# Transposing the second chunk's rows on TensorE between projection groups instead of by DMA

## The chip, the cores and the metric

The kernel runs on one core of a Trainium2 chip. The metric is the device time of one execution in microseconds (us). A profile also gives the span from the first to the last instruction; in these runs the time is about 1.8 us above the span (810.66 against 808.9 for the profiled execution of before). The record marks an execution as slow when it is over 1.5% above the fastest of the same kernel.

## The reference, cut to what matters

A block of a transformer: `h = x + attention(layernorm(x)) @ wo`, then `h + down(gate(layernorm(h)) * up(layernorm(h)))`, on 2048 rows of 1024 elements in bf16. Only its start matters:

```python
m = jnp.mean(x, axis=-1); v = jnp.var(x, axis=-1)
xn = (x - m) / jnp.sqrt(v + 1e-5)
qkv = xn @ wqkv                      # [2048,1024] @ [1024,3072]
# sliding, dilated attention over 8 positions follows, then wo, then the feed-forward part
```

## The kernel before

The 2048 rows are handled in four chunks of 512, each of four row tiles of 128. The projection needs the normalized rows transposed, with the feature on the partitions (`lnT`). Chunk 0, at the very start, transposes on TensorE. Chunks 1 to 3 use DMA transposes from the issue queue of SyncE (SP):

```python
class Norm1:
    def stat(self, t):       # VectorE bn_stats; ScalarE log and exp give 1/sqrt(v + eps)
        stats(xtiles[self.c][t], self.mv4, t)
        rstd_of(self.mv4, self.rs4, t, t + 1)
    def norm(self, t):       # VectorE: one tensor_scalar, bf16 row tile
        self.lns[t] = normalize(xtiles[self.c][t], self.mv4, self.rs4, t)
    def transpose(self, t):  # SP: DMA transpose, 128x1024
        ...                  # c = self.c; allocates lnTs[c] at the first row
        nc.sync.dma_start_transpose(lnTs[c][:, :, bass.ts(t, 128)], self.lns[t][:])
```

Side work like this, and attention, is put into generators. After each projection group (8 matmuls, 1.73 us) a small scheduler adds 1.73 us of credit, at most 4 in all, and runs side work until the credit is spent. That fixes the program order on every engine.

```python
def qkv(c, blocks, last=False):
    for b in blocks:
        for j in range(4):
            ps = psum.tile([128, TC], F32, tag="mm", ...)     # 8 banks, handed out in turn
            mm_group(ps, wts["qkv", b], j, lnTs[c])
            evac_qkv(c, b * 4 + j, ps)                        # ScalarE copies, SP stores q, k, v
            bg.step(GROUP_US)
...
bg.add(rows_gen(norm1[1], True))     # chunk 1: statistics, normalization, DMA transposes
rows2 = rows_gen(norm1[2], False)    # chunk 2: its DMA transposes come below
bg.add(rows2)
...
qkv(0, range(1, 4))                  # 12 groups of chunk 0
load_qk(0)
bg.finish(rows2)
for t in range(4):
    norm1[2].transpose(t)
xtiles[3] = load_x(3, "x", nc.sync)
pump(6)                              # weights of blocks 4 and 5
bg.add(stats_gen(norm1[3]), bg.now + 6.0)
start_attention(0)
qkv(1, range(4))                     # needs all of chunk 1's lnT
qkv(0, range(4, 6))
...
```

## Time and profile before

| what | value |
|---|---|
| time, median of the first 3 runs | 808.54 us (808.07 to 808.65) |
| span and mean granted clock of the profiled execution (its time: 810.66) | 808.9 us, 0.996 |
| idle time of TensorE ahead of chunk 1's first group | 4.26 us |
| granted clock from 42 to 50 us | 0.60 |

"Busy" counts an engine's instructions and not its waits; "PE" is TensorE, "PEld" its weight load, "DVE" VectorE, "ACT" ScalarE, "POOL" GpSimd, and "SPq" the issue of DMAs on SyncE. `L379` is line 379 of the kernel. In a group's row the idle time before it stands after the second bar, with what ended it. The lines themselves are in the prediction.

### The profile page before, as it was taken

The page shows a single profiled execution, that of the slowest core. Times are in us where ns is not written, and L with a number is a line of the kernel's source. Part 1 is how long each engine was busy: PE and PEld are TensorE (multiplying, and loading weights), DVE is VectorE, ACT ScalarE, POOL GpSimd, SP SyncE. Part 2 cuts the span into 40 slices and gives each one's busy share as a digit, 9 for nine tenths or more (in the row PEclk, how much of TensorE's full clock was granted, in tenths as well). Part 3 has the DMA queues.
Part 4 walks back from the last instruction along what each step waited for, and adds up shares of the span by engine and source line. Part 5 has one row for each costly group of instructions (what it writes and reads, how often), then busy time and mean ns, then how long its engine had stood idle before and what let it go on. Part 6 is the DMA issues. An engine that isn't in the chain of part 4 may idle for free.

```text
span 808.9 us, 9878 instructions
## 1 busy us (share of the span) xinstructions
PE 794.0 (98%) x3700; PEld 410.3 (51%) x3769; DVE 552.1 (68%) x580; ACT 254.3 (31%) x562; POOL 165.3 (20%) x160
## 2 busy tenths in 40 slices
PE   8889999999999999999999999999999999999998
PEld 5334444444444444444444444466666666644445
DVE  6519999999899998998989926645646556311111
ACT  4516445323333321013333100244555555400000
POOL 0000000200002000010000010597867778000000
PEclk9989999999999999999999999999999999999999
DMA  7998693897956869667637596542313233466500
GB/s 261 249 268 201 167 269 88 265 288 197 330 172 214 286 243 213 213 216 239 202 105 237 172 245 178 130 121 62 104 53 105 68 90 98 158 208 191 179 27 27
DMA packets 195200, 144.32 MB, mean 178 GB/s; under 512 B 83408, under 2 KB 187984, under 8 KB 193104
## 3 DMA queue, kind: packets, MB, share of 16 engines
q1 hardware_dynamic: 191568, 121.66, 53.7%
q0 software_dynamic: 3584, 22.02, 8.3%
q8 instruction: 30, 0.49, 0.3%
q14 instruction: 18, 0.15, 0.1%
HBM read 114.29 MB, written 22.02 MB: 169 GB/s over the span
## 4 chain that ended last, share of the span: by engine, by line
PE 89%; DVE 7%; DMA 2%; issue 1%; ACT 0%; SPq 0%; DVEq 0%
PE ps L379 18%; PE acc L558 15%; PE pg L379 12%; PE pu L379 12%; PE wo L500 7%; PE pz L609 6%; PE py L609 6%; PE px L609 6%; PE pv L609 3%; PE accl L548 3%; DVE pv L462 2%; DMA lnT<-ln 1%; DVE pv L470 1%; PE ps L341 1%; DVE oD L472 1%
## 5 line engine op out<-in xcount | busy, mean ns | idle before, releaser
L379 PE MATMUL ps<-lnT,w_qkv 128*128 128x512 bf16 x721 | 161.3, 383 | 5.2 <-DMA lnT<-ln 4.3
L379 PEld LDWEIGHTS <-w_qkv 128*128 128x128 bf16 x736 | 72.6, 99 | 93.3 <-issue 8.6
L379 PE MATMUL pg<-lnT,w_wg 128*128 128x512 bf16 x439 | 105.0, 379 | 0.5
L379 PE MATMUL pu<-lnT,w_wu 128*128 128x512 bf16 x439 | 104.9, 379 | 0.4
L558 PE MATMUL acc<-w_wd,gs 128*128 128x512 bf16 x439 | 96.7, 379 | 0.5
L540 DVE TENSOR_TENSOR h<-acc,h 128x512 bf16<-128x512 f32 x28 | 17.4, 682 | 91.1 <-PE acc L558 91.1
L290 ACT CAST sg<-ps 128x512 bf16<-128x512 f32 x96 | 55.0, 587 | 68.9 <-PE ps L379 65.4
L462 DVE TENSOR_TENSOR pv<-vD,at 128x4096 bf16<-128x4096 bf16 x32 | 72.5, 2286 | 0.3
L419 DVE TENSOR_TENSOR prod<-qD,kD 128x4096 bf16<-128x4096 bf16 x32 | 72.3, 2283 | 0.1
L379 PEld LDWEIGHTS <-w_wu 128*128 128x128 bf16 x448 | 43.8, 98 | 52.9
L558 PEld LDWEIGHTS <-gs 128*128 128x128 bf16 x448 | 43.8, 98 | 52.9
L379 PEld LDWEIGHTS <-w_wg 128*128 128x128 bf16 x448 | 43.8, 98 | 52.9
L525 ACT CAST gs<-pg 128x512 bf16<-128x512 f32 x56 | 32.9, 588 | 100.0 <-PE pg L379 96.6
L500 PE MATMUL wo<-w_wo,oT 128*128 128x512 bf16 x251 | 55.6, 379 | 0.3
L474 POOL DMA_DIRECT2D od<-oD x4 | 2.2, 542 | 253.1 <-DVE oD L472 253.1
L609 PE MATMUL px<-lnT,w_pair 128*128 128x512 bf16 x210 | 52.5, 380 | 1.0
L585 POOL TENSOR_TENSOR sw<-w_pair 128x512 fp32r<-128x512 bf16 x28 | 36.5, 1304 | 75.6 <-DMA w_pair<-in_B_w_gate_dram 43.3
L530 ACT CAST us<-pu 128x512 bf16<-128x512 f32 x56 | 32.8, 587 | 57.5 <-PE pu L379 54.1
L500 PEld LDWEIGHTS <-oT 128*128 128x128 bf16 x256 | 25.1, 98 | 30.2
L181 ACT ACTIVATE rs<-mv,eps 128x1 f32<-128x1 f32 x32 | 9.5, 296 | 95.5 <-DVE mv L178 91.9
L587 POOL TENSOR_TENSOR sw<-w_pair 128x512 fp32r<-128x512 bf16 x28 | 36.9, 1319 | 0.0
L421 DVE TENSOR_TENSOR prod<-prod 128x4096 bf16<-128x4096 bf16 x16 | 36.6, 2288 | 0.3
(127 smaller groups left out, 1057.9 us busy)
## 6 DMA issues: line engine op xcount, KB each, us to landing
w_wd<-in_B_w_down_dram SPq DMA_DIRECT2D x32, 896.0 KB, 6.3
w_wg<-in_B_w_gate_dram SPq DMA_DIRECT2D x14, 1024.0 KB, 7.1
w_wu<-in_B_w_up_dram SPq DMA_DIRECT2D x14, 1024.0 KB, 5.5
w_wo<-in_A_wo_dram SPq DMA_DIRECT2D x8, 1024.0 KB, 8.0
w_pair<-in_B_w_gate_dram SPq DMA_DIRECT2D x14, 512.0 KB, 4.0
w_pair<-in_B_w_up_dram SPq DMA_DIRECT2D x14, 512.0 KB, 5.3
w_qkv<-in_A_wqkv_dram SPq DMA_DIRECT2D x5, 1024.0 KB, 10.9
kd<-sg SPq DMA_DIRECT2D x32, 144.0 KB, 3.1
```

Source lines behind the costliest of these rows:

```text
L290: nc.scalar.copy(sg[:, HB:HB + TC], ps[:])
L379: nc.tensor.matmul(ps[:], lhsT=wt[:, ko, bass.ts(j, 128)], rhs=rhs[:, ko, :], start=(ko == 0), stop=(ko == KO - 1))
L419: nc.vector.tensor_tensor(prod[:, j], qD[:], kD[:, :, o:o + SUB], ALU.mult)
L421: nc.vector.tensor_tensor(prod[:, :, 0:16], prod[:, :, 0:16], prod[:, :, 16:32], ALU.add)
L462: nc.vector.tensor_tensor(pv[:, j], vD[:, :, o:o + SUB], at[:, w, None, :].to_broadcast((128, DH, SUB)), ALU.mult)
L500: nc.tensor.matmul(ps[:], lhsT=oTs[c][:, kk, t, :], rhs=wts["wo", c, hf][:, kk, :], start=(kk == 0), stop=(kk == KO - 1))
L525: nc.scalar.copy(gs[:], pg[:])
L530: nc.scalar.copy(us[:], pu[:])
L558: nc.tensor.matmul(acc[t][:], lhsT=hT[f][:, bass.ts(t, 128)], rhs=wts["wd", c, hf, b][:, j, :], start=(f == 0), stop=(f == NF - 1))
L585: nc.gpsimd.tensor_tensor(sw[:, 0], a21, a22, ALU.add)
L587: nc.gpsimd.tensor_tensor(sw[:, 2], a11, a21, ALU.subtract)
L609: nc.tensor.matmul(ps[:], lhsT=lhs[:, ko, :], rhs=rhs[:, ko, :], start=(fresh and ko == 0), stop=(ko == 3), skip_group_check=not fresh)
```

## The change

The intent is to take the second chunk's input off the DMA queues, which are busy with stores and loads at that time, and to put it on TensorE, which runs in program order and whose transposes can't be held up by a queue. Each row tile becomes 8 transposes of 128x128 into two banks, one copied out by ScalarE and one by VectorE, one scheduler step after the row's normalization or later.

```diff
+        def transpose_on_array(self, t):
+            ...
+            for hf in range(2):
+                pt = psum.tile([128, KO // 2, 128], BF, tag="mm", name=f"ptb{c}_{t}_{hf}")
+                for kk in range(KO // 2):
+                    nc.tensor.transpose(pt[:, kk, :], self.lns[t][:, bass.ts(4 * hf + kk, 128)], ident[:])
+                copy = nc.vector.tensor_copy if hf else nc.scalar.copy
+                copy(lnTs[c][:, bass.ts(hf, 4), bass.ts(t, 128)], pt[:])
-    def rows_gen(n, transposed):
-        for t in range(5):
+    def rows_gen(n, on_array):
+        for t in range(6):
             if t < 4:
                 n.stat(t)
                 yield 1.5
-            if t > 0:
+            if 0 < t < 5:
                 n.norm(t - 1)
-                if transposed:
-                    n.transpose(t - 1)
                 yield 0.55
+            if t > 1 and on_array:
+                n.transpose_on_array(t - 2)
+                yield 0.45
```

## The prediction

> **What bounds the kernel now.** The page says where to look: TensorE is busy almost everywhere.
>
> ```profile
> PE 794.0 (98%) x3700; PEld 410.3 (51%) x3769; DVE 552.1 (68%) x580; ACT 254.3 (31%) x562; POOL 165.3 (20%) x160
> ```
>
> So only TensorE's own work or its idle time can move the end. Next I read the groups of instructions, for the idle time ahead of TensorE and who ended it. The last columns are busy us, mean ns of one, then idle us and releasers.
>
> ```profile
> L379 PE MATMUL ps<-lnT,w_qkv 128*128 128x512 bf16 x721 | 161.3, 383 | 5.2 <-DMA lnT<-ln 4.3
> ```
>
> That is the only sizeable idle time on TensorE after the start: 4.3 us, once, ended by a DMA transpose into the normalized input. No other TensorE row has more than 1.5 us. Then the stretches around it (busy us of each engine, granted clock, DMA share, GB/s):
>
> ```profile
> 36.00:42.00 6.00, 2.22 (x11) 0.78 (x8) 0.55 (x1) 3.07 (x13) 0.00 (x0) 0.96 1.03 221
> 42.00:50.00 8.00, 7.30 (x21) 2.83 (x23) 0.55 (x1) 1.17 (x2) 0.54 (x1) 0.60 1.29 211
> 50.00:60.00 10.00, 9.95 (x47) 4.51 (x46) 2.75 (x6) 1.67 (x4) 0.00 (x0) 1.00 1.02 301
> ```
>
> TensorE is idle for four of the six microseconds up to 42, and the eight after them run at a mean clock of 0.60. So the wait costs twice: the idle time, and a slow restart. The chain that ended last, in order of time (start, us, what), has the same place:
>
> ```profile
> 34.18 8.05 DMA lnT<-ln
> 42.48 2.29 PE ps L379 x5
> 44.99 12.39 PE ps L379 x49
> 57.44 10.74 PE ps L379 x49
> ```
>
> Five matmuls take 2.29 us there. In full stride a piece of 50 (one record missing) advances 10.79 us, which is 0.2158 us each. The fourth transpose of the second chunk was issued at 34.2 and took 8.1 us to land (the first three took 3.1 to 3.6), since it shares busy queues with the stores of q and k. The second chunk's first projection group waits for it.
>
> **The size of the hole.** The last group of chunk 0's first three blocks ends at 38.22 (the timeline's piece starts at 17.34 and lasts 20.88). The first output-projection matmul starts at 169.67. Between them the program has 24 groups of chunk 1, 8 of chunk 0, 24 of chunk 2 and 16 of chunk 3, which is 72 groups of 8, or 576 matmuls; 576 x 0.2158 = 124.3 us. The stretch lasts 131.45 us. The excess is 7.15 us: 4.26 idle and 2.9 of slow clock. This is all there is to win.
>
> **What the Trainium skill says.** "TensorE: Matmul & The Clock Gate", section "What's actually happening", says that TensorE falls to half clock after an idle window of about 3.4 us, and needs about as long of sustained work to return. The trace agrees: idle for 4.26 us, then matmuls 0.43 us apart until about 48.4. The same page, "Part 4: PE-mode transpose", says that transposes don't count as busy for this gate. The prologue of this kernel speaks for harmlessness here: it puts bursts of eight transposes between matmuls, and from 10 to 18 us the granted clock is 1.00. "VectorE: DVE Perf Modes", section "The three transpose paths", gives 390 ns for a 128x128 transpose on TensorE and 1309 by DMA. In a pipelined burst this trace shows far less on TensorE, and that is the duration I use. "PSUM — Partial Sum Buffer", "Specifications (TRN2)", counts 8 banks; this kernel's pool has 8 and hands them out in turn, which matters below.
>
> **The change part by part.** Removed: four DMA transposes between 28.2 and 42.2, and with them the wait, the slow clock, and the hold of their row buffers (VectorE lost 9.0 us in three waits for those). Gain on the path: 7.15 us.
>
> Added: 4 x 8 transposes on TensorE, all in line with matmuls, so all on the path. The prologue does the very same:
>
> ```profile
> 14.49 0.61 PE L331 MATMUL pt<-ident,ln 128*128 128x128 bf16 x8
> 14.92 0.59 ACT L333 COPY lnT<-pt 128x512 bf16<-128x512 bf16 x1 [1.07 <-PE pt L331]
> 14.94 2.56 PE L341 MATMUL ps<-lnT,w_qkv 128*128 128x128 bf16 x40
> 15.14 0.42 DVE L336 COPY lnT<-pt 128x512 bf16<-128x512 bf16 x1 [0.71 <-PE pt L331]
> ```
>
> From 14.49 to the next matmul at 14.94 is 0.45 us for eight, so 4 x 0.45 = 1.8 us more TensorE work. The copies, 4 x 0.59 on ScalarE and 4 x 0.42 on VectorE, lie beside the matmuls: ScalarE has about 0.6 to 1.0 us of work per 1.73 us group. They do delay what stands behind them.
>
> Where do they land? I played the scheduler that mixes side work between groups by hand (1.73 of credit gained per group; 1.5 spent per row's statistics, 0.55 per normalization, 0.45 per transposed row). Row 0 is transposed after group 4, row 1 after group 5, rows 2 and 3 after group 6. In VectorE's program order the statistics of row 3 now stand behind the copy of row 0, which waits for TensorE, and the normalizations of rows 2 and 3 behind those. In the kernel before, VectorE ran them ahead of TensorE:
>
> ```profile
> 22.68 1.28 DVE L177 BATCH_NORM_STATS2 st<-x 128x6 f32<-128x512 bf16 x2
> 23.99 0.21 DVE L178 BATCH_NORM_AGGREGATE mv<-st 128x2 f32<-128x12 f32 x1
> 24.11 0.49 DVE L186 TENSOR_SCALAR ln<-x,mv,rs 128x1024 bf16<-128x1024 bf16 x1
> ```
>
> From these statistics to the end of that normalization is 24.11 + 0.49 - 22.68 = 1.92 us. In the changed kernel (an estimate from these rows) group 4 ends at 24.24, 0.2 before its eviction at 24.44 in the timeline. Row 0's transposes start there; VectorE's copy starts 0.65 later, as in the prologue (14.49 to 15.14), at 24.9; the statistics of row 3 at about 25.25, row 2 is normalized by 27.2, and row 3, after the copy of row 1 and its own ScalarE step, by about 28.1. TensorE reaches row 2 at 24.24 + 2 x (0.45 + 1.73) = 28.6. So TensorE doesn't wait, by about half a microsecond. The banks don't hold it either: a transposed row takes 2 of 8, and the allocation eight back is always an eviction at least two groups old. The second chunk is complete at about 31; its first group starts at 38.22 + 1.8 = 40.0.
>
> Sum: -7.15 + 1.8 = -5.35, from 808.54 to 803.2.
>
> **The rivals.** (1) VectorE takes over as the bound. It is busy almost without a break from 57.2, when the fourth chunk's rows land, to 190, so only an earlier start moves it. Those rows are loaded behind the stores of k and chunk 2's transposes on the same issue queue (issue from 50.2, landing 7.0 us later). In the changed kernel the last k store can't be issued before its group has ended, near 40.0, and been copied, 41.0, which puts the rows' issue near 48 instead of 50.2. So VectorE moves up by only some 2.3 us, TensorE by 5.35. What TensorE needs of it next: the attention output of chunk 0 (last piece issued at 156.7, 6.8 to landing, so 163.5; used at 169.67; slack 6.2) and the second normalization of chunk 0 (last transpose issued at 189.8, 3.2 to landing, so 193.0; first used at 197.3; slack 4.3). The last becomes 4.3 - 5.35 + 2.3 = 1.25. If VectorE didn't move at all, TensorE would wait 1.05 there: 804.3. Later VectorE is ahead again (in the feed-forward part it waits 17 times, 11.2 us in all, for ScalarE's copies of TensorE's results), so the lag isn't carried on. (2) The row normalizations come late and TensorE waits for them in order, after group 6. With half a microsecond of margin, a stall of 1 us is well possible: 804.2. (3) The slow clock comes anyway, because the transposes count as idle: 2.9 us kept, 806.1. The longest stretch is 0.9 us (rows 2 and 3), against 0.45 in the prologue; unlikely. (4) The wait for the transpose is replaced by a wait for weights: blocks 4 and 5 of the projection are issued at 52.9 and land 10.9 and 12.9 us later, at 63.8 to 66.6. Before, the first is used at 42.48 + 2.9 + 128 x 0.2158 = 73.0, now at 67.6, and its issue moves up as well. No stall. (5) The transpose's wait is hidden anyway: no, it is in the chain and the idle time is TensorE's.
>
> **The range and the chances.** The middle is 803.3, a tenth over the sum for rivals 1 and 2. Below, hardly more than the whole 7.15 less 1.8 is to be had, and repeats of the kernel before spread 0.6 us: 802.2. Above, rivals 1 and 2 together give about 805.3, so 805.6 leaves them in. Two per cent is 16 us, more than twice the hole, so faster by that much is practically excluded; slower would need a new wait of over 21 us, which nothing here suggests.
>
> **What would show it.** Right: no idle time on TensorE ahead of the second chunk's first group, clock 1.00 from 36 to 50, 32 more small matmuls of 0.056 us apart near 24 to 30, chunk 1 starting near 40.0, the first output-projection matmul near 164.3 and the rest shifted as a block. Wrong: idle time before the transposes ended by a normalization, before the first gate matmul (near 192) ended by a transpose, or before the output projection; or a clock under 1.00 after the transposes. If that first gate matmul comes 5.35 earlier but the end doesn't, a later wait that no row shows today has taken the gain.

## The result, and the profile after

The changed kernel takes 804.84 us (median of 4, 804.5 to 806.28) against 808.6 of before (median of 4, 808.07 to 810.99). Ratios here and below are taken over the fast runs of the same rounds, so not quite the ratio of the medians. This one is 0.9956, with a 95% interval of 0.9936 to 0.9975: 3.8 us faster by the medians. The number lies inside the predicted range (802.2 to 805.6); the middle, 803.3, was 1.5 too low.

The page of the changed kernel, and its row of projection matmuls:

```profile
PE 797.9 (99%) x3801; PEld 411.8 (51%) x3801; DVE 553.0 (69%) x584; ACT 255.4 (32%) x566; POOL 165.3 (21%) x160
L391 PE MATMUL ps<-lnT,w_qkv 128*128 128x512 bf16 x736 | 159.7, 379 | 0.0
```

The idle time behind the second bar, 5.2 us before, is 0.0. The stretches of the changed kernel (busy us of PE, PEld, DVE, ACT and POOL, then the granted clock, DMA share and GB/s):

```profile
36.00:42.00 6.00, 6.00 (x29) 2.74 (x28) 1.22 (x4) 3.55 (x12) 0.00 (x0) 1.00 0.76 163
42.00:50.00 8.00, 8.00 (x39) 3.63 (x37) 0.00 (x0) 1.77 (x4) 0.54 (x1) 1.00 1.12 230
50.00:60.00 10.00, 10.00 (x48) 4.49 (x46) 5.59 (x13) 1.97 (x7) 0.00 (x0) 1.00 0.93 265
```

TensorE is busy throughout, at a clock of 1.00. Hole and slow restart are gone together. The chain of the changed kernel through the same place (start, us, what):

```profile
17.16 6.91 PE ps L391 x32
24.06 0.45 PE ptb L234 x8
24.51 1.73 PE ps L391 x8
26.24 0.45 PE ptb L234 x8
26.68 1.73 PE ps L391 x8
28.41 0.89 PE ptb L234 x16
29.30 30.86 PE ps L391 x143
```

Transposes stand where the hand-played scheduler put them, after groups 4, 5 and 6. Eight take 0.45 us, and nothing but TensorE is on the chain. The timeline of the changed kernel (start, us, engine, line, operation) shows the step that was tightest:

```profile
24.55 0.42 DVE L236 COPY lnT<-ptb 128x512 bf16<-128x512 bf16 x1 [2.13 <-PE ptb L234]
24.89 1.27 DVE L177 BATCH_NORM_STATS2 st<-x 128x6 f32<-128x512 bf16 x2
27.07 0.54 DVE L186 TENSOR_SCALAR ln<-x,mv,rs 128x1024 bf16<-128x1024 bf16 x1
28.25 1.06 PE L234 MATMUL ptb<-ident,ln 128*128 128x128 bf16 x16
```

VectorE does wait for TensorE in its copy, as predicted, and the last row is normalized at 27.61, 0.64 us before TensorE reaches rows 2 and 3 at 28.25. So TensorE doesn't wait.

To see where the time went I split each profiled span into three parts: the start of the first full projection matmul; the stretch from there to the first output-projection matmul, less its 672 matmuls of 0.2158 us (145.02 us), which I call the loss; and the rest.

| profiled execution | start | loss | rest | span |
|---|---|---|---|---|
| before | 17.34 | 7.32 | 639.22 | 808.9 |
| changed | 16.99 | 1.81 | 639.07 | 802.9 |

The loss goes from 7.32 to 1.81, a gain of 5.51. (The prediction's 7.15 counts from the modelled end of a matmul instead of a start, hence 0.17 less.) The other 0.5 us between the two spans is chance at the start and in the rest. So the two profiles differ by about the predicted 5.35, while the two sets of timed runs differ by 3.8. That gap is what the experiments were for.

### The profile page after: what moved, and what is told of

It is laid out like the page before. It is cut to its first block, busy times and chain, and to the rows that moved or that the text cites. A ratio compares the mean times of both kernels' runs of the same rounds, so it can differ in the third digit from the quotient of the medians.

```text
span 802.9 us, 10008 instructions
## 1 busy us (share of the span) xinstructions
PE 797.9 (99%) x3801; PEld 411.8 (51%) x3801; DVE 553.0 (69%) x584; ACT 255.4 (32%) x566; POOL 165.3 (21%) x160
## 4 chain that ended last, share of the span: by engine, by line
PE 98%; DMA 1%; SPq 0%; DVE 0%; issue 0%
PE acc L570 21%; PE ps L391 20%; PE pu L391 12%; PE pg L391 12%; PE wo L512 7%; PE pz L621 7%; PE py L621 7%; PE px L621 6%; PE pv L621 3%; PE accl L560 3%; PE ps L353 1%; DMA w_qkv<-in_A_wqkv_dram 1%; PE ptb L234 0%; PE pt L343 0%; SPq L269 0%; SPq L272 0%
## 5 line engine op out<-in xcount | busy, mean ns | idle before, releaser
L621 PE MATMUL px<-lnT,w_pair 128*128 128x512 bf16 x224 | 55.6, 381 | 0.0
```

Of the source, the lines that this page charges most:

```text
L621: nc.tensor.matmul(ps[:], lhsT=lhs[:, ko, :], rhs=rhs[:, ko, :], start=(fresh and ko == 0), stop=(ko == 3), skip_group_check=not fresh)
```

## The experiments

The first set of four ran on one chip, the second and third on two others. Each has its own 11 timed executions of before beside it. Their medians were 808.45, 809.68 and 810.95. Theory A says that the profiled execution of before was one of its slower ones; theory B says that the change costs more than its 1.8 us of transposes.

### same: the kernel before against itself

No edit.

> The kernel before, unchanged, against itself, to see how its own time varies. The predicted gain was 5.35 us, the timed one 3.76. Theory A: the profiled execution of before (span 808.9, clock 0.996, time 810.66) was one of its slower ones. The wait of about 4.3 us comes every time, but the slow clock after it (2.9 us) only in some executions[...]. Then the spans of this run's executions fall into two groups, near 806.5 (clock 0.998 or more) and near 809 (clock near 0.996), and their mean is near the timed 808.6 less 1.8. Theory B: the wait and the slow clock come every time and the changed kernel costs more than 1.8 us: then all spans are 808.5 to 809.3 with clock 0.996.

Measured: 809.91 us median (808.18 to 811.52, 6 runs), ratio 1.0009 (0.9981 to 1.0037). The times of its six executions and of the 11 of before beside it, with the mean granted clock:

```
same:   808.18 (0.998) 808.36 (1.000) 808.55 (1.000) 811.27 (0.997) 811.52 (0.996) 811.52 (0.996)
before: 806.17 (1.000) 807.20 (0.998) 807.67 (0.997) 807.75 (0.997) 808.35 (1.000) 808.45 (0.998)
        810.43 (0.998) 810.98 (0.996) 811.49 (0.996) 811.72 (0.996) 811.97 (0.996)
```

Here they fall into two groups with nothing between 808.6 and 810.4, and the upper one mostly has the lower clock. (The two groups are no law: beside the second set four of the 11 executions of before lie between 809.3 and 809.9.) What holds is that before's time spreads over 5.8 us by itself (806.17 to 811.97), and the time of the first profile, 810.66, is in the upper part. That is theory A. The profile of this kernel shows a wait that is not the same as in the first profile (first line, who waited for what: us in total, times, longest; second line, the stretch from 42 to 50 as above):

```profile
PE ps L379 <- DMA kd<-sg: 5.4, 1, 5.4
42.00:50.00 8.00, 5.74 (x20) 2.26 (x21) 0.55 (x1) 1.06 (x2) 0.00 (x0) 0.79 1.24 234
```

The wait is 5.4 us here, and the loss is 7.19 (7.02 counted as the prediction counts), so 1.6 us of slow clock. (The releaser named is the transfer that came last by the records; it is a store of k. The fourth transpose was issued just ahead of it and took 9.1 us to land.) The size of the hole is thus no constant: it depends on when one transfer lands in busy queues, and on how long the slow clock lasts after the wait. By the mean clock from 42 to 50 us, 0.79 here and 0.60 in the first profile, that is about 3.4 us and 6.4 us at half clock, where matmuls come 0.43 us apart instead of 0.2158 (an estimate: 8 x 0.21 / 0.5 and 8 x 0.40 / 0.5), though the wait is the longer one here.

### keep_warm: idle matmuls inside the wait

```diff
     start_attention(0)
+    fill = psum.tile([128, 512], F32, tag="mm", name="fill_ps")
+    for i in range(16):
+        nc.tensor.matmul(fill[:], lhsT=warm[:, 0:128], rhs=warm[:], start=True, stop=True)
     qkv(1, range(4))
```

> Before, with 16 idle matmuls (16 x 0.2158 = 3.45 us) put on TensorE between the last group of chunk 0 and the first of chunk 1, inside the wait of 4.26 us. The DMA transposes stay. Theory A (the slow clock is a result of the idle time, on top of it): idle time falls below 1 us, the clock stays at 1.00 from 42 to 50, and every execution is as fast as before's fastest: spans 805.7 to 806.5, 0.5 to 2 us below before's mean and with less spread. Rival (the clock is low for another reason, or its slowness is absorbed): spans as before, 806.5 to 809. If the idle time, and not the clock, were all that the change wins, this kernel would show no gain at all.

Measured: 809.63 us median (808.46 to 810.4), ratio 1.0003 (0.9976 to 1.0031), the clock 0.999 or 1.000 in all six. The granted clock from 42 to 50 is 1.00 in this kernel's profile; that stretch, and the waits of TensorE:

```profile
42.00:50.00 8.00, 7.44 (x35) 3.45 (x36) 0.55 (x1) 2.10 (x4) 0.54 (x1) 1.00 1.27 212
PE ps L379 <- ACT sg L290: 1.6, 1, 1.6
PE ps L379 <- DMA lnT<-ln: 1.3, 1, 1.3
```

The slow clock is indeed a result of the idle time: filling the wait removes it. But the time did not fall: the spans are 806.6 to 808.5, so my expectation of 805.7 to 806.5 failed and the rival's 806.5 to 809 came. TensorE now came sooner to a second wait that was not in the profile of before: for ScalarE's eviction of a bank, at 65.0 us.

### doubled: each transpose made twice

```diff
-                for kk in range(KO // 2):
+                for kk in [*range(KO // 2)] * 2:
                     nc.tensor.transpose(pt[:, kk, :], ...)
```

> The changed kernel with each of its 32 transposes on TensorE made twice into the same place. If their cost is wholly on the path, as predicted (0.45 us per 8), the time is 1.8 us above the changed kernel's 804.84: 806.6, ratio to before about 0.998. If they cost less (hidden in idle time), it is 804.8 to 805.5; if theory B holds and a row on TensorE costs twice what I took, 808 or more.

Measured: 806.54 us median (806.41 to 807.07), ratio 0.9969 (0.9945 to 0.9993). That is 1.70 us above the changed kernel's 804.84 (a different set of runs) and in its profile the loss is 3.60 against 1.81. The chain shows rows 2 and 3:

```profile
29.31 1.79 PE ptb L234 x32
```

So a transpose costs 0.056 us on the path, wholly and no more, and theory B is out. The clock stayed at 1.00 even through rows 2 and 3, which are now 1.8 us of transposes without a matmul between.

### last_row: only row 3 on TensorE

```diff
                 n.norm(t - 1)
+                if on_array and t < 4:
+                    n.transpose(t - 1)
                 yield 0.55
-            if t > 1 and on_array:
-                n.transpose_on_array(t - 2)
+            if t == 5 and on_array:
+                yield "later", 3.0
+                n.transpose_on_array(3)
                 yield 0.45
```

> Rows 0 to 2 of the second chunk by DMA as before (they landed at 31.4, 33.4 and 36.4, ahead of the need at 38.2), only row 3, the one that the wait was for, on TensorE. If the wait is the fourth transfer's alone, the whole gain stays at a quarter of the cost: 3 x 0.45 = 1.35 us below the changed kernel, so about 803.5, no idle time before the second chunk. Rival: one of the first three transfers, still queued among the stores, becomes the last to land and the wait comes back at 1 to 4 us: 805 to 808.

Measured: 808.78 us median (805.67 to 809.36), ratio 0.9986 (0.9959 to 1.0013): the expected 803.5 failed, though the wait for the transposes is gone. The timeline of this kernel shows the second wait in full:

```profile
45.78 0.59 ACT L305 CAST sg<-ps 128x512 bf16<-128x512 f32 x1 [1.14 <-PE ps L394]
57.59 1.28 DVE L177 BATCH_NORM_STATS2 st<-x 128x6 f32<-128x512 bf16 x2 [20.45 <-DMA x<-in_A_x_dram]
59.16 0.29 ACT L181 ACTIVATE rs<-mv,eps 128x1 f32<-128x1 f32 x1 [12.79 <-DVE mv L178]
62.38 0.57 ACT L305 CAST sg<-ps 128x512 bf16<-128x512 f32 x1
63.00 3.22 PE L394 MATMUL ps<-lnT,w_qkv 128*128 128x512 bf16 x8 [3.44 <-ACT sg L305]
```

Read it from the top. The first line is the last eviction before the stop. The fourth chunk's rows land at 57.6; VectorE had waited 20 us for them. ScalarE's small instruction on their variance stands in program order ahead of the next evictions, and waits 12.8 us for VectorE. Meanwhile no bank is emptied. Eight banks hold 8 x 1.73 = 13.8 us of TensorE's work, and that is used up: TensorE waits 3.4 us. A DMA load thus stops TensorE by way of two engines. In the changed kernel's timeline the same chain is there, and it just holds:

```profile
46.61 0.59 ACT L302 CAST sg<-ps 128x512 bf16<-128x512 f32 x1 [1.14 <-PE ps L391]
54.27 1.28 DVE L177 BATCH_NORM_STATS2 st<-x 128x6 f32<-128x512 bf16 x2 [16.12 <-DMA x<-in_A_x_dram]
59.05 0.57 ACT L302 CAST sg<-ps 128x512 bf16<-128x512 f32 x1
```

From one eviction to the next are 12.4 us, against 13.8 of banks. The margin is less than the difference: an eviction starts some 0.2 us after its group ends and takes 0.57 us before the bank is free, so about 0.6 us is left (an estimate). The same count for last_row, from the eviction at 45.78 to the one at 62.38, gives a wait of 16.6 + 0.8 - 13.8 = 3.6 us, where the profile has 3.44.

### again: the changed kernel once more

No edit.

> The changed kernel again, on one chip with the next three, for its spread. The 17 executions of before beside the first four experiments ran from 806.17 to 811.97 (mean 809.5), so the 3.76 first measured rests on a lucky handful of before. Theory A: changed near 804.7, most executions within 0.5 us of it, 4 to 5 us below the mean of before on the same chip (ratio 0.994 to 0.996), with single executions 1 to 2 us up, where a second wait shows: the fourth chunk's rows land late, VectorE's statistics wait for them, ScalarE waits in order for these, its evictions stop and TensorE runs out of banks. Theory B (the gain is 3.8 and the rest was never there): ratio 0.9956 or above.

Measured: 805.09 us median (804.91 to 805.33, 5 runs), ratio 0.9941 (0.9927 to 0.9954), so 4.6 us by the medians. The loss in its profile is again 1.81. There was no outlier this time.

### after_later: the fourth chunk's statistics five groups later

```diff
-    bg.add(stats_gen(norm1[3]), bg.now + 6.0)
+    bg.add(stats_gen(norm1[3]), bg.now + 15.0)
```

> The changed kernel with the fourth chunk's statistics put five groups later in program order (ready 15 us instead of 6 us after the first 12 groups), so that ScalarE has evicted more groups before it comes to wait for them. Theory A: no execution is slowed by banks; same fast level (804.5 to 804.9), no outlier over 805.3. Rival (the outlier near 806.3 has another source, say the clock at the start): the outliers stay.

Measured: 807.18 us median (806.17 to 809.08), ratio 0.9968 (0.9953 to 0.9983): 2.1 us slower than the changed kernel beside it. The expectation failed. The loss in the profile is 1.81, so the front is untouched; the rest is 1.1 us longer. TensorE waits 0.9 us at 486 us, for the attention output of the last chunk. The store of that output (engine, operation, out<-in) is issued in this kernel at

```profile
469.54 0.56 POOL L486 DMA_DIRECT2D od<-oD  x1 [102.69 <-DVE oD L484]
```

and in the changed kernel at

```profile
450.74 0.56 POOL L486 DMA_DIRECT2D od<-oD  x1 [87.57 <-DVE oD L484]
```

My edit made the scheduler lose credit (it keeps no more than 4 us while nothing is ready), so attention fell behind in program order until the end, by 19 us at the last chunk. The profiled execution was the fastest of six; that the slower ones have more of the same is likely and not shown.

### last_row_later: only row 3 on TensorE, later statistics

The edits of last_row and after_later together.

> Only row 3 on TensorE, as in the run before of that idea, and the fourth chunk's statistics five groups later. That run had no wait for a transpose, but a wait of 3.4 us for ScalarE's eviction, near 60 us. If this second wait was all that hid the gain, it is gone: 803.3 (the changed kernel's 804.7 less 3 x 0.45), 1.3 to 1.4 us below the changed kernel, ratio to it 0.998. If instead DMA traffic with three transposes left keeps the rows of the fourth chunk so late that another wait appears: 804.5 or more.

Measured: 804.77 us median (804.32 to 805.89), ratio 0.9939 (0.9924 to 0.9953), level with the changed kernel beside it (805.09). The wait for ScalarE is gone and the loss is 0.47, a quarter of 1.81 as it should be. But the edit has after_later's drawback: 1.2 us of wait at 485 us for the last chunk's attention output.

### keep_warm_later: idle matmuls and later statistics

The edits of keep_warm and after_later together.

> Before with the 16 idle matmuls in the wait, and the later statistics. The last such run had no slow clock, but lost 1.6 us to the eviction wait. With that gone, what is left is the wait itself (4.3 to 5.4 us) without the slow clock: 801.1 (the changed kernel less its 1.8 us of transposes, an estimate of the time with neither) plus 4.3 to 5.4, so 805.4 to 806.5 and little spread, some 3 us below before's mean. If it stays at 808.5 or more, the slow clock wasn't a cost of its own.

Measured: 809.69 us median (807.84 to 811.04), ratio 0.9995 (0.9978 to 1.0012), clock 1.000 in all six. The profiled execution is the fastest of the six (span 806.0, the others 806.5 to 809.3). In it the transposes had landed before the idle matmuls ended, so the loss is just the 3.48 of these, and a wait of 0.9 us stands at 488 us, once more from the later statistics. Expected 805.4 to 806.5, so missed, and by the test in the text above (808.5 or more) it counts against a cost of the slow clock. I don't take it as settled, since the edit's own cost is in it (after_later: 2.1 us by the medians); but what made five of the six executions slower than the profiled one was not traced.

### last_row_x3: only row 3 on TensorE, an earlier load

```diff
+    xtiles[3] = load_x(3, "x", nc.sync)
     for t in range(4):
         norm1[2].transpose(t)
-    xtiles[3] = load_x(3, "x", nc.sync)
```

(on top of last_row). The text below takes the late attention output for that of chunk 0; the trace, read again, shows it at 485 us, which is chunk 3, as told above. I had misread it.

> Only row 3 on TensorE, and the fourth chunk's rows loaded ahead of the third chunk's four DMA transposes on the issue queue instead of behind them. The later statistics had only moved the trouble: VectorE starts attention when these rows have landed (57.0 in that run), and the attention output then reached TensorE 1.2 us late. If this chain (rows landed, 92 us of VectorE work, output stored and loaded again) is what limits once TensorE is faster, loading the rows earlier starts VectorE near 50, both waits go, and the time is 803.3 to 803.5, 1.4 below the changed kernel's 804.7 to 805.1, ratio to before 0.9925. Rival: the early load lands in the same busy queues and delays the first chunk's q and k or a row's transpose instead; then 804.5 or more.

Measured: 803.63 us median, ratio 0.9939 (0.9903 to 0.9974), but four executions at 802.48, 803.41, 803.51 and 803.74, and two at 808.77 and 811.9. The profile fell on the slowest, and shows why that one is slow:

```profile
PE ps L394 <- DMA w_qkv<-in_A_wqkv_dram: 5.5, 1, 5.5
```

The rows now land at 47.0 and the wait for ScalarE is gone, but the weights of block 4 stand behind rows and transposes on the issue queue. The four issues of the transposes took 20.5 us (45.15 to 65.63), so the weights were issued at 65.7, landed at 71.8 and came 5.5 us late, and the slow clock comes with that wait: the loss is 8.98.

### keep_warm_x3: idle matmuls, an earlier load

The edits of keep_warm and last_row_x3's load on before.

> Before with the 16 idle matmuls in the wait, and the early load of the fourth chunk's rows. The two runs with idle matmuls kept the clock at 1.00 but lost what that gave to later waits (an eviction, the attention output). If those waits come from the late rows, they are gone here and what remains is the wait for the transposes: 801.1 plus 4.3 to 5.4, so 805.4 to 806.5, 3 to 4 us below before, with little spread. If it is 808.5 or more again, the late rows weren't the reason, or the slow clock is no cost of its own.

Measured: 808.06 us median, ratio 0.9983 (0.9956 to 1.001): three executions at 806.64, 806.79 and 807.09, all with clock 1.000, three at 809.03, 811.07 and 812.27. The profile is of the fast kind: no wait at all, loss 3.48, which is the 16 idle matmuls. The slow kind was not traced; late weights as in last_row_x3 would fit. The expected 805.4 to 806.5 was missed, by the fast kind too, if only by 0.1 to 0.6 us. Its control, before_x3, has the slow clock in its profile and is no slower (mean 808.1 against 808.8).

### before_x3: the earlier load alone

The load of last_row_x3 on before.

> Before with the early load alone, as the control of the two above. In before the profile shows no wait on TensorE behind the late rows, so theory A expects no change but chance: ratio 0.998 to 1.002, with the slow clock (0.996) still there in part of the executions. Rival: part of before's own spread (806 to 812) is the late rows too; then it is 1 to 3 us faster and evener.

Measured: 807.89 us median (806.63 to 810.25), ratio 0.9969 (0.9949 to 0.9989). Faster than I expected, by 2.5 us in the mean. Its profile has a wait of 2.8 us and a loss of 4.65, because the fourth transpose landed 6.4 us after its issue, not 8.1 or 9.1. Yet the early load is issued at 44.4, after that transpose had landed, so I can't see how it could have helped it. Whether this is chance or an effect stays open.

### reorder_x3: no transpose on TensorE, another order

```diff
-    pump(4)
+    pump(5)
     xtiles[2] = load_x(2, "x", nc.sync)
+    pump(6)
...
     load_qk(0)
+    xtiles[3] = load_x(3, "x", nc.sync)
+    qkv(0, range(4, 6))
+    load_v(0)
     bg.finish(rows2)
     for t in range(4):
         norm1[2].transpose(t)
-    xtiles[3] = load_x(3, "x", nc.sync)
-    pump(6)
...
     qkv(1, range(4))
-    qkv(0, range(4, 6))
-    load_v(0)
```

> No transpose on TensorE at all: before with chunk 0's last two projection blocks moved ahead of chunk 1's (their weights loaded ahead of the third chunk's rows, which aren't needed soon), and the early load of the fourth chunk's rows. The second chunk's DMA transposes then have 13.8 us more before they are needed. If the wait is a matter of order alone, it is gone at no cost on TensorE: 801.1 plus at most 0.5, 3 to 4 us below the changed kernel, ratio to before 0.990. Rival: the moved weights come too late (wanted at 38.2 instead of 73) or push the third chunk's rows or the stores back, and a wait of 2 to 5 us appears in another place: 804 to 807.

Measured: 811.73 us median (810.09 to 813.05), ratio 1.0012 (0.9994 to 1.003), where I expected 0.990. The weights of block 4 are now loaded ahead of chunk 2's rows. The front is perfect: a loss of 0.02. And the time is lost again, near the end:

```profile
PE wo L501 <- DMA oT<-od: 5.4, 1, 5.4
```

Attention of chunk 0 starts eight groups later in program order in this edit, the credit is capped, and the last chunk's attention output is stored at 476.7 instead of 450.7; TensorE waits for it at 489, and the clock falls once more (0.995).

## Why the prediction was right, and where it was off

The range held, both times (804.84 and 805.09), and so did the forecast of no change by 2%. The mechanism was right, but that the number fell inside the range is in part luck: the range reached up to 805.6 to leave room for rivals 1 and 2, which did not come, and that room took up an error of the sum. By its own steps:

- **The hole, 7.15 us, is all there is to win.** Right for the execution profiled (a loss of 7.32, of which 1.81 is left), wrong as the size for the median. Here the sum failed: it took 5.35 us, read from an execution that lasted 810.66, off a median of 808.54 of other executions, and took their spread for 0.6 us, from three of them, where 11 executions spread over 5.8. Taken off 810.66 it gives 805.3, within 0.5 of both medians. In the profiles of before, same and before_x3 the rest is 639.22 to 639.23 and the loss 7.32, 7.19 and 4.65, so it is mainly the hole that varies. The median hole is smaller (worked out from the times, not traced): from the first timing 808.6 - (804.84 - 1.8) = 5.6 us, from the second 809.68 - (805.09 - 1.8) = 6.4. The term of the sum that was mis-sized is this one.
- **The slow clock is a second cost of the wait.** The mechanism is shown: with the wait filled by idle matmuls the clock stayed at 1.00 (keep_warm), and it fell in every profile with an idle gap of 2.8 us or more on TensorE after the start, and in none with 1.6 us or less. Its size in the profiles varies: 2.9 us in the first, 1.6 in same. In timed runs its cost is not shown: keep_warm and keep_warm_later met other waits, and keep_warm_x3 was no faster than its control.
- **Transposes cost 1.8 us, all on the path.** Right: a loss of 1.81 in three profiles (the changed kernel twice, and after_later), 3.60 with twice as many, 0.47 with a quarter.
- **Where they land, and that TensorE doesn't wait for the rows.** Right. The statistics of row 3 were put at 25.25 and came at 24.89 in a profile that began 0.35 earlier; TensorE's margin was 0.64 us.
- **Rival 1, VectorE.** Didn't happen; the estimate behind it was right with two errors that cancelled. The fourth chunk's rows were not issued near 48 but at 51.25, since the third chunk's transposes took 10.3 us of issue; but they began to land 3.0 us later instead of 7.0, and VectorE moved up by 2.9, not 2.3. The second normalization of chunk 0 kept 1.45 us (190.0 against 191.45), predicted 1.25. For the attention output of chunk 0 I had set the last piece against the first use; the first piece is what counts: slack 9.8 before and 2.5 after (landed 161.36, used 163.82).
- **Rivals 2 to 5.** None came. Rival 3 in particular: the clock was 1.00 after 0.9 us of transposes, and after 1.8 in doubled. In rival 4 the weights' issue did not move up as I said (53.29 against 52.85), but they landed in time, at 60.7; in last_row_x3 that rival came.
- **What I missed altogether:** the wait of ScalarE, in order, for the fourth chunk's statistics. In the changed kernel it holds with about 0.6 us to spare. A change that gained more at the front (last_row, by 1.35) or ran TensorE ahead without moving the DMA queue (keep_warm) ran into it. The single slow execution of the changed kernel (806.28) may be that; it was not traced.
- **Why the fourth transpose is slow.** The prediction says: because it shares busy queues with the stores of q and k. No run took the stores away, so this stays an inference. Shown is that the fourth is the one that matters: with it alone on TensorE the wait is gone (last_row, last_row_later).

No version beat the changed kernel for sure. Four of six executions of last_row_x3 were at least 1.3 us below its 805.09 (measured on another chip), two were 4 to 7 us above it.

## What to carry to other kernels

One profile is one execution: where a kernel's executions scatter by more than the gain in question, subtract a hole only from the time of the execution in which it was measured, or measure the hole several times. A wait for a transfer in busy queues is replaced well by work on the engine that waits, at a cost that can be read off an earlier use of the same instructions. When the busy engine gets ahead, look for what stands in program order before its evictions on another engine, count its banks in microseconds, and check what an edit does to a scheduler that fixes the order of everything after it.

## What the Trainium skill lacked or had wrong

- "VectorE: DVE Perf Modes", "The three transpose paths", gives 390 ns for a 128x128 transpose on TensorE. No page gives the time of one in a stream of them. Here that is 56 ns (0.45 us for eight, and the loss of 1.81 us for 32), which decides whether it pays.
- "DMA: Bandwidth & Descriptors", "DMA Transpose (X-bar)", gives no time to landing among other traffic. Here a 128x1024 transpose landed in 3.1 us at best, and the fourth one of the second chunk, issued among stores, in 5.5 to 9.1 us in seven profiles.
- "TensorE: Matmul & The Clock Gate": "What's actually happening" puts the fall of the clock after an idle window of about 3.4 us. In before_x3 it fell after 2.8 us of idle time (mean clock 0.79 from 42 to 50); after 1.6 us in keep_warm it did not. And "Part 4: PE-mode transpose" doesn't say how many transposes in a row are harmless to it: here 1.8 us of them left it at 1.00.
